# Cutting the last output block of a GeGLU kernel at 384 + 128 columns instead of 256 + 256

## Chip, cores, metric

One core of a Trainium2 chip. The metric is the device time of one execution in microseconds (us). A kernel is timed in rounds beside the kernel before on the same chip. A ratio is the mean time of one kernel's fast runs over the mean of the other's fast runs in the same rounds, so it is not quite the ratio of the medians that I quote; its 95% interval stands in brackets. Each run is marked fast or slow, by its time and the clock granted to TensorE.

## The reference

```python
# x: [32, 32, 1024]   w_gate, w_up: [1024, 3584]   w_down: [3584, 1024], bfloat16
def reference(x, w_gate, w_up, w_down):
    return (_gelu(x @ w_gate) * (x @ w_up)) @ w_down     # gelu in its tanh form
```

So there are 1024 tokens. A first product makes the gated hidden tensor `gT` (3584 x 1024, kept in SBUF). A second product multiplies it by `w_down`.

## The kernel before

The change touches the second product only. Each output block is 128 tokens by 512 columns. Its sum runs over 28 tiles of 128 rows: 28 pairs of a weight load (of a `gT` tile) and a matmul (which streams columns of `wd`). Then VectorE casts the block from PSUM to bfloat16, and SyncE (SP in the profile) issues a store. There are 8 x 2 blocks, and the very last one is already cut into two halves of 256 columns.

```python
    def mm2_block(tsl, dsl):
        out_ps = pspool.tile([P, dsl.stop - dsl.start], fp32, name="out_ps", tag="acc")
        for ft in range(FT):                                  # FT = 28
            nc.tensor.matmul(out_ps, lhsT=gT[:, ft, tsl], rhs=wd[:, ft, dsl],
                             start=(ft == 0), stop=(ft == FT - 1))
        o_sb = opool.tile([P, DB], bf16, name="o_sb", tag="o_sb")[:, : dsl.stop - dsl.start]
        nc.vector.tensor_copy(o_sb, out_ps)
        nc.sync.dma_start(out=of[tsl, dsl], in_=o_sb)

    for tt in range(NT):                                      # NT = 8, NDB = 2, DB = 512
        tsl = slice(tt * P, (tt + 1) * P)
        for db in range(NDB):
            if tt == NT - 1 and db == NDB - 1 and DB % 2 == 0:
                q = DB // 2
                for i in range(2):
                    mm2_block(tsl, slice(db * DB + i * q, db * DB + (i + 1) * q))
            else:
                mm2_block(tsl, slice(db * DB, (db + 1) * DB))
```

(Loads, warm-up matmuls and the first product with its elementwise work are cut; the change doesn't touch them.)

## Time and profile before

| | before |
|---|---|
| device time, median of the first 3 runs | 301.06 us (300.96 to 301.46) |
| span of the profiled execution | 298.9 us |
| first weight load of the second product | 198.24 us |
| first matmul of the last 512 columns to the last landing | 8.32 us |
| last landing to the end of the span | 1.42 us |

From the page of the kernel before, the span and the busy time of each engine:

```profile
span 298.9 us, 3462 instructions
...
PE 294.6 (99%) x1381; PEld 135.4 (45%) x1381; DVE 108.2 (36%) x241; ACT 97.6 (33%) x170; POOL 0.2 (0%) x4
...
PE 99%; DVE 0%; issue 0%
PE gate_ps L107 33%; PE out_ps L182 32%; PE up_ps L107 32%; PE warm_ps L73 1%; DVE o_sb L190 0%
```

PE is TensorE's matmuls and PEld its weight loads, which overlap them. The last two lines are the chain of work that ended last. It is TensorE nearly throughout. The Trainium skill warns ("Perfetto Trace Analysis", Identifying the Most-Contended Engine) that the busy share of matmuls is not a good measure of how close a kernel is to its limit, because matmuls are pipelined. This trace shows the pipelining: one matmul of 512 columns is recorded with 379 ns while the next starts 216 ns after it. (The section says that pipelined instructions look smaller in a trace; here the record is longer than the step.) I therefore work with start times.

The end of the kernel, grouped by shape (busy us, mean ns of one, then idle time before and who ended it), window 285 us to the end:

```profile
L182 PEld LDWEIGHTS <-gT 128*128 128x128 bf16 x74 | 7.2, 98 | 3.0
L182 PE MATMUL out_ps<-wd,gT 128*128 128x256 bf16 x56 | 6.3, 272 | 0.0
...
L190 DVE CAST o_sb<-out_ps 128x256 bf16<-128x256 f32 x2 | 0.8, 425 | 5.0 <-PE out_ps L182 5.0
L190 DVE CAST o_sb<-out_ps 128x512 bf16<-128x512 f32 x1 | 0.7, 693 | 5.4 <-PE out_ps L182 5.4
```

The cast waits for PE; no wait of PE for a cast is recorded. After the last matmul, the chain in order of time (start us, duration us), same kernel:

```profile
295.00 0.10 PEld L182 LDWEIGHTS <-gT 128*128 128x128 bf16 x1
295.42 0.42 DVE L190 CAST o_sb<-out_ps 128x256 bf16<-128x256 f32 x1 [2.63 <-PE out_ps L182]
295.87 0.33 SPq L191 DMA_DIRECT2D out_dram<-o_sb  x1
```

The last store of before, with its size and the time from issue to landing (the median that the view gives is of this one store):

```profile
out_dram<-o_sb SPq DMA_DIRECT2D x1, 64.0 KB, 1.6
```

Only what follows the last matmul is exposed: the cast, the issue of the store, its landing, and the closing work. This stretch is what the change is after.

### The profile page before, as it was taken

To read this page: it belongs to the slowest core of one execution; us is meant where nothing else is said; L and a number is where in the kernel's file an instruction comes from. 1 tells how busy PE (TensorE), PEld (TensorE's weight loads), DVE (VectorE), ACT (ScalarE), POOL (GpSimd) and SP (SyncE) were. 2 spreads that over 40 slices of the span, in tenths; PEclk is the share of its full clock that TensorE was granted. 3 is DMA by queue.
4 is the path that set the end of the run, shared out by engine and by line. 5 is a ranking of instruction groups with operands and counts; after the bars stand their busy time and mean duration, and the time that the engine had idled before them with its cause. 6 is when DMAs were issued, how large, how long until landed. Compare 5 with 4: busy or idle time off the path is not lost.

```text
span 298.9 us, 3462 instructions
## 1 busy us (share of the span) xinstructions
PE 294.6 (99%) x1381; PEld 135.4 (45%) x1381; DVE 108.2 (36%) x241; ACT 97.6 (33%) x170; POOL 0.2 (0%) x4
## 2 busy tenths in 40 slices
PE   8999999999999999999999999999999999999995
PEld 3444444444444444444444444444444444444454
DVE  0067654455554455554445554440010001000101
ACT  1086545544544544544544544530000000000000
POOL 0000000000000000000000000000000000000000
PEclk9999999999999999999999999999999999999999
DMA  7999996080026006200800000000001000100010
GB/s 175 265 305 378 377 365 246 1 279 3 0 83 197 2 0 190 91 2 1 277 5 2 0 0 2 0 0 18 20 18 35 18 20 18 35 20 18 18 35 21
DMA packets 29168, 26.44 MB, mean 88 GB/s; under 512 B 9056, under 2 KB 25568, under 8 KB 29152
## 3 DMA queue, kind: packets, MB, share of 16 engines
q1 hardware_dynamic: 28880, 25.96, 27.8%
q10 hardware_dynamic: 272, 0.26, 0.3%
q8 instruction: 11, 0.18, 0.2%
q14 instruction: 5, 0.04, 0.1%
HBM read 22.02 MB, written 2.10 MB: 81 GB/s over the span
## 4 chain that ended last, share of the span: by engine, by line
PE 99%; DVE 0%; issue 0%
PE gate_ps L107 33%; PE out_ps L182 32%; PE up_ps L107 32%; PE warm_ps L73 1%; DVE o_sb L190 0%
## 5 line engine op out<-in xcount | busy, mean ns | idle before, releaser
L107 PE MATMUL gate_ps<-xT,wg 128*128 128x512 bf16 x448 | 106.6, 380 | 0.0
L107 PE MATMUL up_ps<-xT,wu 128*128 128x512 bf16 x448 | 106.3, 379 | 0.0
L182 PE MATMUL out_ps<-wd,gT 128*128 128x512 bf16 (+1 forms) x476 | 96.9, 366 | 0.0
L182 PEld LDWEIGHTS <-gT 128*128 128x128 bf16 x476 | 46.6, 98 | 50.4
L107 PEld LDWEIGHTS <-wg 128*128 128x128 bf16 x448 | 43.9, 98 | 53.7 <-issue 1.1
L107 PEld LDWEIGHTS <-wu 128*128 128x128 bf16 x448 | 43.8, 98 | 52.9
L117 ACT ACTIVATE h<-gate_ps 128x512 bf16<-128x512 f32 x56 | 33.4, 597 | 54.9 <-PE gate_ps L107 54.8
L125 ACT ACTIVATE s<-z 128x512 bf16<-128x512 bf16 x56 | 35.3, 630 | 45.9 <-DVE z L123 45.9
L127 DVE TENSOR_TENSOR hu<-h,up_ps 128x512 bf16<-128x512 bf16 x56 | 38.2, 682 | 16.6 <-ACT h L117 16.6
L121 DVE TENSOR_SCALAR w<-sq 128x512 bf16<-128x512 bf16 x56 | 16.4, 294 | 74.3 <-ACT sq L119 74.3
L190 DVE CAST o_sb<-out_ps 128x512 bf16<-128x512 f32 (+1 forms) x17 | 11.2, 661 | 84.6 <-PE out_ps L182 84.6
L119 ACT ACTIVATE sq<-gate_ps 128x512 bf16<-128x512 f32 x56 | 33.1, 592 | 0.0
L128 DVE TENSOR_TENSOR gT<-hu,s 128x512 bf16<-128x512 bf16 x56 | 23.8, 426 | 10.5 <-ACT s L125 10.4
L123 DVE TENSOR_TENSOR z<-w,h 128x512 bf16<-128x512 bf16 x56 | 23.8, 425 | 1.8
L73 PE MATMUL warm_ps<-const-bfloat16-1.0 128*128 128x512 bf16 x9 | 4.0, 626 | 0.8 <-PEq L216 0.8
L73 PEld LDWEIGHTS <-const-bfloat16-1.0 128*128 128x128 bf16 x9 | 1.2, 137 | 2.7 <-issue 2.7
L117 ACT ACT_TABLE_LOAD x1 | 1.3, 1283 | 1.2 <-PEq L216 1.2
L125 ACT ACT_TABLE_LOAD x1 | 1.3, 1283 | 0.0
L216 POOL MEMSET const-bfloat16-1.0<- 128x1 bf16 x1 | 0.1, 102 | 0.0
L216 POOL MEMSET const-uint8-127<- 128x1 uint8 x1 | 0.1, 102 | 0.0
L216 POOL MEMSET const-float32-0.0<- 128x1 f32 x1 | 0.1, 99 | 0.2 <-issue 0.2
L216 POOL MEMSET const-float32-1.0<- 128x1 f32 x1 | 0.1, 99 | 0.0
## 6 DMA issues: line engine op xcount, KB each, us to landing
wd<-in_w_down_dram SPq DMA_DIRECT2D x7, 1024.0 KB, 12.6
wg<-in_w_gate_dram SPq DMA_DIRECT2D x6, 1024.0 KB, 5.2
wu<-in_w_up_dram SPq DMA_DIRECT2D x6, 1024.0 KB, 7.4
out_dram<-o_sb SPq DMA_DIRECT2D x15, 128.0 KB, 1.7
wu<-in_w_up_dram SPq DMA_DIRECT2D x4, 256.0 KB, 4.7
wg<-in_w_gate_dram SPq DMA_DIRECT2D x3, 256.0 KB, 4.7
wg<-in_w_gate_dram ACTq DMA_DIRECT2D x1, 256.0 KB, 2.9
out_dram<-o_sb SPq DMA_DIRECT2D x2, 64.0 KB, 2.0
```

The costliest lines, as they stand in the source:

```text
L73: nc.tensor.matmul(warm_ps, lhsT=ones_w, rhs=ones_m, start=True, stop=True)
L107: nc.tensor.matmul(ps, lhsT=wt[:, dt, :], rhs=xT[:, dt, t0 : t0 + tw], start=(dt == 0), stop=(dt == DT - 1),)
L117: nc.scalar.activation(h, gate_ps, ACT.Copy)
L119: nc.scalar.activation(sq, gate_ps, ACT.Square)
L121: nc.vector.tensor_scalar(w, sq, _C2A, _C2, ALU.mult, ALU.add)
L123: nc.vector.tensor_tensor(z, w, h, ALU.mult)
L125: nc.scalar.activation(s, z, ACT.Sigmoid)
L127: nc.vector.tensor_tensor(hu, h, up_ps, ALU.mult)
L128: nc.vector.tensor_tensor(gT[:, ft, t0 : t0 + tw], hu, s, ALU.mult)
L182: nc.tensor.matmul(out_ps, lhsT=gT[:, ft, tsl], rhs=wd[:, ft, dsl], start=(ft == 0), stop=(ft == FT - 1),)
L190: nc.vector.tensor_copy(o_sb, out_ps)
L216: nc = _bacc.Bacc("TRN2", target_bir_lowering=False, num_devices=1)
```

## The change

Its intent: make the last piece small, so that less cast and less store stand after the last matmul. The sum of columns is the same.

```diff
-            if tt == NT - 1 and db == NDB - 1 and DB % 2 == 0:
-                q = DB // 2
-                for i in range(2):
-                    mm2_block(tsl, slice(db * DB + i * q, db * DB + (i + 1) * q))
+            if tt == NT - 1 and db == NDB - 1 and DB > P:
+                cut = (db + 1) * DB - P
+                mm2_block(tsl, slice(db * DB, cut))
+                mm2_block(tsl, slice(cut, (db + 1) * DB))
```

The order of instructions on every engine stays; only shapes change: the widths of the last two runs of 28 matmuls, of their two casts and of their two stores.

## The prediction

> **What bounds the kernel now.** TensorE. The profile's engine table has PE busy 294.6 us of a 298.9 us span (99%), and the chain of waits is 99% PE, 32% of it the second product (out_ps). The granted clock is 1.0. Busy time overcounts overlapping matmuls, so I use starts: 512-column matmuls start every 216 ns and the 256-column ones of the last two blocks every 109.2 ns. That is N/2.4 + 2.5 ns, the warm spacing that the Trainium skill states ("TensorE: Matmul & The Clock Gate", Back-to-back issue gap); this trace agrees at both widths.
>
> The only exposed part is the tail. Instruction times before: last matmul starts at 295.112 us; the cast of 128x256 starts 0.31 us later and takes 0.425; the store is issued at 295.874, its first packet moves at 296.705, the last landing is at 297.431; closing work to 298.85.
>
> **What the change does.** Still 476 matmuls and loads, 17 casts and stores. The last block goes from 256+256 to 384+128 columns. Nothing before 289.1 us changes. No wait is added: the 384 block's cast and store issue finish before the last cast is due.
>
> Costs, as estimates from the measured spacing and durations:
> - Matmul stream: 28 x 162.5 + 27 x 55.8 ns to the last start against 55 x 109.2 ns: +0.05 us, provided that 128-column matmuls do stream at 55.8 ns.
> - End of the last matmul: 0.273 us falls to about 0.219: -0.05.
> - Last cast: 0.692 (512) and 0.425 (256) give 1.04 ns a column, so 0.29 for 128: -0.13.
> - Last store: 32 KB instead of 64 KB, 8 packets per DMA engine at about 17 ns instead of 27: -0.08 at best. Rows of 256 bytes fall under the 512-byte size that the skill names for full DMA rate ("DMA: Bandwidth & Descriptors", Specifications), so this may be lost.
>
> Sum: -0.2 us.
>
> **The risk: weight loads.** Each matmul needs its own weight load, whose record lasts 98 ns, longer than 55.8. If loads could not overlap each other, spacing would be about 100 ns and the last block 1.2 us longer: net +1.0 us. I think it is mostly latency: one warm load, after an idle PE near 18.9 us, is followed by its matmul 5 ns later and by the next load 15 ns later; at the start a cold load is followed by its matmul after 31 ns. So I give about 65-70% to spacing of 56 to 65 ns, the rest to 75 to 105 ns.
>
> **Prediction:** 300.9 us, range 300.4 to 301.9. Faster by over 2%: 0.5%; within 2%: 99%; slower by over 2%: 0.5%. The largest change I can argue for is 1 us, 0.4%.
>
> **What would show each step.** Right: 128-column matmuls start 55-65 ns apart; the last one starts near 295.2 us; the last cast is 0.29 us; last cast start minus last matmul start falls from 0.31 to about 0.26; the store from issue to last landing takes 1.5 us or less (1.56 before). Wrong: loads about 98 ns apart and the last matmul starting near 296.3 us; or a store clearly above 1.6 us; or a last cast not shorter.
>
> **What would make it wrong.** Loads that bound the last 28 matmuls; 256-byte rows landing slowly; an instruction fetch transfer (one of 16 KB stood at 293.1 us) falling in front of the last store; or run-to-run variation, as large as the effect (301.0 to 301.5 in the three runs).

## The result, and the profile after

First timing: after 300.88 us median (300.75 to 301.17, 6 runs), before 301.29 us (300.96 to 301.88, 6 runs), ratio 0.9986 [0.9973, 0.9999]. Within 2%, and within the predicted range.

From the page of the kernel after:

```profile
span 298.9 us, 3436 instructions
...
PE 293.4 (98%) x1355; PEld 134.3 (45%) x1381; DVE 108.1 (36%) x241; ACT 97.6 (33%) x170; POOL 0.2 (0%) x4
...
PE 97%; DMA 1%; issue 1%; DVE 0%
```

26 matmul records are missing (1355 of 1381), while all 1381 weight loads are there. The profile loses such records now and then; the lower PE share is no finding. I count with weight loads where it matters.

The end of the kernel after, grouped by shape, 285 us to the end:

```profile
L182 PEld LDWEIGHTS <-gT 128*128 128x128 bf16 x75 | 6.2, 98 | 4.3
...
L182 PE MATMUL out_ps<-wd,gT 128*128 128x384 bf16 x28 | 4.7, 326 | 0.0
L182 PE MATMUL out_ps<-wd,gT 128*128 128x128 bf16 x28 | 1.7, 219 | 0.0
...
L190 DVE CAST o_sb<-out_ps 128x384 bf16<-128x384 f32 x1 | 0.6, 558 | 3.9 <-PE out_ps L182 3.9
L190 DVE CAST o_sb<-out_ps 128x128 bf16<-128x128 f32 x1 | 0.3, 291 | 1.0 <-PE out_ps L182 1.0
```

And in order of time:

```profile
294.74 1.63 SPq L191 DMA_DIRECT2D out_dram<-o_sb  x2
294.79 0.89 PE L182 MATMUL out_ps<-wd,gT 128*128 128x128 bf16 x13
294.96 0.54 PEld L182 LDWEIGHTS <-gT 128*128 128x128 bf16 x9
295.72 0.29 DVE L190 CAST o_sb<-out_ps 128x128 bf16<-128x128 f32 x1 [1.01 <-PE out_ps L182]
```

The SPq line covers both store issues, the last one from 296.03 us. That last store:

```profile
out_dram<-o_sb SPq DMA_DIRECT2D x1, 32.0 KB, 1.4
```

Thirteen matmuls of 128 columns take 0.89 us, of which the last one's own duration is 0.22: the twelve steps between them are 56 ns each. The weight loads are recorded with 98 ns and start 56 ns apart, so they overlap one another.

Notice that both spans read 298.9 us, though the time fell. The lines of the second product's weight loads (count, duration ns min/median/max, first and last start in us), before:

```profile
L182 PEld LDWEIGHTS <-gT x476: 97/98/98, 198.2 to 295.0; 128*128 128x128 bf16 x159
```

and after:

```profile
L182 PEld LDWEIGHTS <-gT x476: 97/98/98, 198.5 to 295.4; 128*128 128x128 bf16 x159
```

In the profiled execution of after the second product began 0.29 us later, before any changed instruction. What the change did is therefore read from the tail, the stretch from the first matmul of the last 512 columns on. These are instruction times of the traces, in us:

| piece of the tail | before | after | difference | predicted |
|---|---|---|---|---|
| first to last matmul start | 6.004 | 6.058 | +0.054 | +0.05 |
| last matmul start to cast start | 0.310 | 0.257 | -0.053 | -0.05 |
| last cast | 0.425 | 0.291 | -0.134 | -0.13 |
| cast end to store issue | 0.027 | 0.027 | 0 | 0 |
| store issue to last landing | 1.557 | 1.440 | -0.117 | -0.08 at best |
| tail | 8.32 | 8.07 | -0.25 | -0.2 |
| closing work, last landing to end of span | 1.42 | 1.42 | 0 | 0 |

In the 14 traces the second product begins between 197.95 and 198.88 us, whatever the kernel; the standard deviation is 0.29 us. That is the size of the effect, so one timing cannot settle it. A better figure is the time from the first weight load of the second product to the end of the span, which leaves the head (everything before the second product) out. I call it the second part below. It is 100.61 us before and 100.35 us after. Of before there is this one trace; of after there are three, with second parts within 0.02 us of each other though two of them are from different chips.

### The profile page after: what moved, and what is told of

It reads as the page before. It is cut to its first block, busy times and chain, and to the rows that moved or that the text cites. A ratio compares the mean times of both kernels' runs of the same rounds, so it can differ in the third digit from the quotient of the medians.

```text
span 298.9 us, 3436 instructions
## 1 busy us (share of the span) xinstructions
PE 293.4 (98%) x1355; PEld 134.3 (45%) x1381; DVE 108.1 (36%) x241; ACT 97.6 (33%) x170; POOL 0.2 (0%) x4
## 4 chain that ended last, share of the span: by engine, by line
PE 97%; DMA 1%; issue 1%; DVE 0%
PE gate_ps L107 32%; PE out_ps L182 32%; PE up_ps L107 32%; DMA xT<-in_x_dram 1%; DVE o_sb L190 0%
## 5 line engine op out<-in xcount | busy, mean ns | idle before, releaser
L182 PE MATMUL out_ps<-wd,gT 128*128 128x512 bf16 (+2 forms) x468 | 96.5, 366 | 0.4
L182 PEld LDWEIGHTS <-gT 128*128 128x128 bf16 x476 | 45.5, 98 | 51.6
L190 DVE CAST o_sb<-out_ps 128x512 bf16<-128x512 f32 (+2 forms) x17 | 11.2, 660 | 84.4 <-PE out_ps L182 79.1
```

## The experiments

Theory A: the time falls because a shorter last piece shortens only what stands exposed after the last matmul. Rival B: the 0.4 us of the first timing is how the heads happened to run. Rival C: the matmul stream decides, and splits only cost. A further rival, on the risk that the prediction named: the 28 short matmuls streamed well only because they were few.

A summary first. "Second part" is as defined above. The device time exceeds the recorded span by about 2 us (time that the trace doesn't show). Every timed run lists its span, so this excess can be had for all runs of a kernel: it averages 1.98 us for before (1.81 to 2.10 over its runs) and differs a little from kernel to kernel. The ratio that the traces give is 1 + (difference of the second part + difference of the mean excess) / 301.

| kernel | tail us | closing us | second part, against before, us | mean excess us | ratio that these give | ratio measured |
|---|---|---|---|---|---|---|
| after (first) | 8.07 | 1.42 | -0.26 | 1.97 | 0.9991 | 0.9986 [0.9973, 0.9999] |
| after_again | 8.08 | 1.42 | -0.24 | 2.02 | 0.9993 | 0.9997 [0.9985, 1.001] |
| after_third | 8.08 | 1.42 | -0.24 | 1.97 | 0.9992 | 0.9987 [0.9976, 0.9999] |
| e1_whole, 512 | 8.66 | 1.13 | +0.04 | 1.86 | 0.9997 | 0.9999 [0.9985, 1.0013] |
| e6_whole_padded, 512 | 8.66 | 1.03 | -0.06 | 1.84 | 0.9993 | 0.9998 [0.9985, 1.0012] |
| e2_reversed, 128 + 384 | 8.51 | 1.42 | +0.18 | 1.98 | 1.0006 | 1.0004 [0.9991, 1.0016] |
| e3_448_64 | 8.50 | 1.42 | +0.18 | 1.94 | 1.0004 | 1.0 [0.9988, 1.0013] |
| e4_store_256 | 8.19 | 1.42 | -0.14 | 2.02 | 0.9997 | 0.9994 [0.998, 1.0008] |
| e7_448_64_act | 8.10 | 1.19 | -0.45 | 2.02 | 0.9986 | 0.9988 [0.9974, 1.0002] |
| e8_448_64_early | 8.05 | 1.43 | -0.19 | 2.17 | 1.0000 | 1.001 [0.9998, 1.0023] |
| e5_all_128 | - | 0.83 | +2.52 | 1.82 | 1.0078 | 1.0077 [1.006, 1.0094] |
| e9_after_merged | 8.08 | 1.12 | -0.55 | 1.89 | 0.9979 | 0.9975 [0.9959, 0.9991] |
| e10_after_merged2 | 8.09 | 0.90 | -0.76 | 2.19 | 0.9982 | 0.9976 [0.9963, 0.9989] |

The ratio that the traces give lies inside the measured interval for every kernel. That is a weak test, since an interval is about as wide as 0.7 to 1 us and so wider than most of the effects; the traces carry the argument. The outputs are right.

### after_again and after_third: the change repeated

No edit.

> The changed kernel once more, so that every later run has it beside it. 'Tail' below is the time from the first matmul of the last 512 output columns to the last landing of the last store: 8.32 us in the profile of before, 8.07 us in the first profile of after. Theory A (a shorter last piece shortens only what is exposed after the last matmul): tail 8.07 us again, within 0.05; time 0.25 us under before. Theory B (the 0.4 us of the first timing is how the head of the kernel happened to run, and the tail adds nothing that is seen): time equal to before within 0.1 us, although the tail is shorter in the profile.

> The changed kernel a third time, for the size of its gain and beside the two merged ones. Theory A: from the first matmul of the second product to the end of the span 0.25 us less than before, as in its other two profiles; time 0.25 us (ratio 0.9992) under before, within noise of about 0.3 us that comes from the head.

Measured: tails of 8.08 and 8.08 us, second part 0.24 us shorter than before both times. Times 301.10 us (before 301.05) and 300.92 us (before 301.18); ratios as in the table. Theory A holds in the traces three times out of three. The timings alone are weaker: the middle one contains "no difference", and all three contain the 0.9991 to 0.9993 that the traces give. The three ratios average 0.9990. Rival B is right only about the size of the first timing: of its 0.4 us, 0.25 is the change by the traces, and the rest I put down to the runs.

### e1_whole: no split

```diff
-                for i in range(2): mm2_block(... 256 columns ...)
+                mm2_block(... 512 columns ...)
```

> The last block in one piece of 512 columns, no split. Theory A: stream to the last start 27 x 216 ns = 5.83 us (0.17 us less than before), then 0.42 us to the cast, cast 0.69, store 1.70 us from issue to landing: tail 8.67 us, so 0.35 us slower than before and 0.60 us slower than after. Theory B: equal to before. A theory C, that the matmul stream decides: 0.17 us faster than before.

Measured: the tail came out as theory A had it, 8.66 us (5.83 to the last start, 0.42, cast 0.69, store 1.70). The end of it, by shape:

```profile
L190 DVE CAST o_sb<-out_ps 128x512 bf16<-128x512 f32 x2 | 1.4, 692 | 10.7 <-PE out_ps L182 10.7
```

But the time was equal to before: 300.95 against 301.05 us, ratio 0.9999. As a forecast of the time this was a miss. The trace shows where most of the 0.34 us came back: the closing work after the last landing took 1.13 us instead of 1.42. The mean excess was 0.12 us smaller too. Theory C falls with the same tail: the stream was 0.18 us shorter than in before, as C had it, and what stood after it grew by 0.52. So the closing work is not a constant, and something other than the tail had changed with the split. That led to e6, and later to e9 and e10.

### e2_reversed: the same pieces, long one last

```diff
-                mm2_block(384 columns); mm2_block(128 columns)
+                mm2_block(128 columns); mm2_block(384 columns)
```

> The same two pieces in reverse order, 128 and then 384: the same matmuls, casts and stores as after, only the last piece is the long one. Theory A: tail 5.95 + 0.36 + 0.56 + 0.03 + about 1.63 = 8.53 us, 0.46 us slower than after and 0.2 us slower than before. A rival, that the gain comes from the kinds of pieces (fewer ns per matmul, cheaper forms) and not from which is last: equal to after.

Measured: tail 8.51 us, against 8.53 expected. The casts of its last three blocks (512, 128 and 384 columns) are

```profile
L190 DVE CAST o_sb<-out_ps x3: 293/558/691, 289.3 to 295.4; 128x512 bf16<-128x512 f32 x1, 128x128 bf16<-128x128 f32 x1, 128x384 bf16<-128x384 f32 x1
```

and the last of them is the one of 384 columns. The second part is 0.44 us longer than in after, with the same set of instructions and the same closing work of 1.42 us. So it is the place of the short piece that counts, not its kind. The time, 301.09 us and ratio 1.0004, lies on the expected side but inside the noise.

### e3_448_64: the cut moved further

```diff
-                384 + 128
+                448 + 64
```

> The cut moved further: 448 and then 64 columns. If weight loads still don't bind at 64 columns: matmuls 29 ns apart, tail 6.09 + 0.23 + 0.23 + 0.03 + about 1.40 = 7.97 us, 0.1 us faster than after. If a weight load needs more than 29 ns of its own (40 ns, say), the last block is 0.3 us longer and the tail about 8.26 us, 0.2 us slower than after. In either case the 448-column piece's cast and store issue end close to when the last piece wants them, so a short wait of the last cast or of the last store issue may show.

Measured: tail 8.50 us, later than either forecast. The two questions came apart. Weight loads still don't bind. These are the groups by shape, from 294.7 to 296 us:

```profile
L182 PE MATMUL out_ps<-wd,gT 128*128 128x64 bf16 x28 | 1.0, 193 | 0.0
L182 PEld LDWEIGHTS <-gT 128*128 128x128 bf16 x28 | 1.0, 98 | 0.2
```

28 loads and 28 matmuls within 1.0 us; in the instruction times they start 29 ns apart, as forecast. The loss is in the store. In order of time:

```profile
295.03 0.62 DVE L190 CAST o_sb<-out_ps 128x448 bf16<-128x448 f32 x1 [4.61 <-PE out_ps L182]
295.69 1.27 SPq L191 DMA_DIRECT2D out_dram<-o_sb  x2
295.85 0.22 DVE L190 CAST o_sb<-out_ps 128x64 bf16<-128x64 f32 x1 [0.19 <-PE out_ps L182]
```

The two issues together occupy SP's queue for 1.27 us: the first took 0.33, the second, 0.42 us after it, 0.85. A 16 KB instruction fetch, one packet, ran from 295.33 to 296.57 us, and the packets of the 448-column store began at 296.52. Its slowest packet took 211 ns, where the same store's slowest in e8 took 49. The last packet ended 0.73 us after the first began, against 0.45 to 0.46 us in e7 and e8. Two explanations were left: the two issues are too close on one queue (Q), or the fetch holds up the stores (F). (That these fetches are PE's I infer from their spacing: about 27.6 us in before, where a load and a matmul start every 216 ns, and 7.15 us in e5_all_128 below, where they start every 55.9 ns. That is about 256 PE instructions a fetch in both.)

### e7_448_64_act and e8_448_64_early: which of the two

```diff
# e7_448_64_act: e3's cut, and the last store from ACT's queue
-        nc.sync.dma_start(out=of[tsl, dsl], in_=o_sb)
+        eng = nc.scalar if tsl.stop == N and dsl.stop == D else nc.sync
+        eng.dma_start(out=of[tsl, dsl], in_=o_sb)
# e8_448_64_early: e3's cut, SP's queue; the first block of the second product in two PSUM halves,
# one store: 56 more PE instructions, so that the fetch comes earlier
```

> 448 and 64 columns, the last store issued from ACT's queue instead of SP's. In e3_448_64 matmuls did run 29 ns apart, but the issue of the last store, 0.42 us after the one before it, took 0.85 us instead of 0.33. Theory Q (two issues close together on one queue): the issue takes about 0.33 to 0.42 us here and the tail is 7.98 us. Theory F (the 16 KB instruction fetch of 1.24 us, which stood there at that time, holds up the store): the issue or the landing is again about 0.5 us late, tail about 8.5 us.

> 448 and 64 columns on SP's queue as in e3_448_64, but the first output block of the second product is also computed in two halves of 256 columns (one store): 56 more instructions on PE, 0.07 us more of matmul stream, so that the last instruction fetch comes earlier than in e3_448_64, by about 28 matmul pairs. Theory F: the fetch is over before the last store, its issue takes 0.33 us, tail 7.98 us. Theory Q: the issue takes 0.85 us again, tail 8.49 us.

Measured in e8_448_64_early: the fetch ran from 289.63 to 290.51 us, long before the end; the issues are again 0.42 us apart on the same queue, and the second took 0.38 us.

```profile
295.09 0.81 SPq L191 DMA_DIRECT2D out_dram<-o_sb  x2
295.26 0.23 DVE L190 CAST o_sb<-out_ps 128x64 bf16<-128x64 f32 x1 [0.19 <-PE out_ps L182]
```

So close issues alone cost 0.05 us, and the 0.5 us needed the fetch: F, in this trace. But a late fetch alone is not enough either. In after_again, after_third and e9_after_merged a fetch overlapped the packets of the 384-column store (slowest 222, 222 and 204 ns), which landed 2.03 to 2.33 us after its issue; yet the last store, issued 1.30 us after that one, landed within 1.44 to 1.45 us of its own issue, as in after. The 0.5 us of e3_448_64 came from the late fetch and the close second issue together. In e7_448_64_act the issue took 0.36 us and the tail was 8.10 us, but there the fetch (294.91 to 295.85 us) had ended before the packets began at 296.13, so that run doesn't separate the two. Whether the late fetch would also hold up a store on another queue stays open.

The trace of before supports F with no edit at all: its store of 292.82 us overlapped a fetch (293.12 to 293.99), its slowest packet took 186 ns, and it landed 2.35 us after issue, where the last store of the same size took 1.56. That landing was not exposed.

Both expected a tail of 7.98 us and got 8.05 and 8.10: the last store's packets began 0.88 to 0.89 us after its issue instead of 0.83, just when those of the 448-column store had ended (11 and 32 ns later). It seems that at 64 columns the last store runs into the one before it (the timing fits, no run tests it), and the 0.1 us that the shorter piece should have brought over after shrank to at most 0.03. The time of e8 was 301.23 us (ratio 1.001), slower than its trace suggests: its excess over the span was 2.13 to 2.22 us in all six runs, 0.19 us above that of before. Why this kernel loses time outside the recorded span I don't know.

### e4_store_256: the store's share alone

```diff
 # matmuls and casts of 384 and 128 columns as in after, into one output tile
-                stores of 384 and 128 columns
+                stores of 256 and 256 columns
```

> Matmuls and casts of after (384 and 128), but the stores cut at 256: the last store carries 64 KB in rows of 512 bytes, as in before. It measures the store's share alone: last store 1.56 us from issue to landing instead of 1.44, the rest of the tail as in after, tail 8.19 us. If short rows cost something at landing, the 1.44 us would be matched or beaten here.

Measured: last store 1.557 us from issue to landing, tail 8.19 us, both as expected. Its two stores:

```profile
out_dram<-o_sb SPq DMA_DIRECT2D x2, 64.0 KB, 1.6
```

The two halves of the gain are thus told apart: 0.117 us of the 0.25 is the smaller store, the rest is the cast (0.134), with the matmul terms cancelling (+0.054 and -0.053). Rows of 256 bytes cost nothing at landing: their packets take 18 ns, those of 512 bytes 27, of 1024 bytes 47.

### e5_all_128: the weight loads, 64 times over

```diff
-                mm2_block(tsl, slice(db * DB, (db + 1) * DB))
+                for c in range(db * DB, (db + 1) * DB, P):
+                    mm2_block(tsl, slice(c, c + P))
```

> Every block of the second product in pieces of 128 columns (64 casts and stores of 32 KB instead of 17): the load question of the prediction, 64 times over. If a weight load streams at 56 ns for good (A): 1792 matmuls x 55.85 ns = 100.1 us instead of 96.9, time 3.2 us over before (ratio 1.011), less the shorter tail. If the 28 matmuls of after ran at 56 ns only because PE's queue held them ready (rival): spacing falls to 80 or 98 ns after the first block, and the time rises by 46 to 79 us.

Measured: 303.58 against 301.18 us, ratio 1.0077 [1.006, 1.0094]. The loads of the second product:

```profile
L182 PEld LDWEIGHTS <-gT x1792: 97/98/98, 198.3 to 298.4; 128*128 128x128 bf16 x200
```

1792 loads in 100.16 us are 55.9 ns each, to the end. The rival is out: the short stream holds without the help of a filled queue. The stream grew by 3.40 us (from 96.76), as forecast within 0.2; the stretch after the last load shrank by 0.88 us, of which 0.59 is closing work, which I had not foreseen.

### e6_whole_padded: what goes with the closing work

```diff
 # e1_whole, and the store of the block before the last issued in two halves of 256 columns
```

> One piece of 512 columns again, with one store of the block before it issued in two halves, so that SP issues 17 stores as in before. In e1_whole the tail was 0.34 us longer than in before (as theory A had it) but the closing work after the last landing took 1.13 us instead of 1.42, and the time was equal. If the closing work goes with the number of instructions on SP (theory S): tail 8.66 us as in e1_whole, closing work 1.42 us, time 0.3 us over before, about 301.4. If it went with the missing split itself: closing 1.13 us and time equal to before.

Measured: tail 8.66 us as in e1_whole, closing work 1.03 us, time 300.92 against 301.04 us (ratio 0.9998). Theory S as I had written it fell, for the closing work did not go back to 1.42. But the padding had not done what I meant. The extra store waits for one semaphore, not two, so SP has 82 traced instructions instead of 83. By that count the traces line up. In before, after, e2, e3, e4 and e8 there are 83 instructions of SP, and in each SP stops between two of its closing instructions. In e1 and e7 there are 81, and the stop stands two closing instructions later. From instruction times (us, SP only; "drain" and "wait" are the trace's DRAIN and EVENT_SEMAPHORE):

```
before (83)              e1_whole (81)            e10 below (79)
297.601  drain           297.917  drain           297.312  drain
298.068  drain  <- stop  297.977  drain           297.381  drain
298.329  wait            298.130  wait            297.534  wait
298.421  drain           298.608  drain  <- stop  297.625  drain
298.790  wait            298.884  wait            298.001  wait
```

The usual step from the first to the second is 0.06 us; here it is 0.47. In e1 the stop falls where SP would wait for other engines in part anyway, which hides some of it.

### e9_after_merged and e10_after_merged2: the closing work moved on purpose

```diff
 # e9: the stores of the first two blocks of the second product merged into one of 256 KB
 # e10: the first four blocks' stores merged in pairs
+            if tt == 0:                    # e10: tt < 2
+                ... both casts into o_big[128, 1024] ...
+                nc.sync.dma_start(out=of[tsl, :], in_=o_big)
```

> after, with the stores of the first two output blocks of the second product merged into one of 256 KB: 16 stores instead of 17, and the same PE instructions as after. Over the runs so far the closing work after the last landing was 1.42 us where the trace has 83 instructions of SP, 1.03 us with 82 and 1.13 to 1.19 us with 81, because one gap of about 0.4 us stands at a fixed place of SP's instruction stream. By that (theory S, mended): 81 instructions here, closing 1.13 us, tail 8.07 us as in after, time 0.3 us under after. If the closing had gone with PE's instructions or with the split: 1.42 us.

> after, with the first four output blocks' stores merged in pairs: 15 stores, 79 instructions of SP. By theory S the gap of SP falls behind the last instruction of the span: closing work at most 1.0 us, tail 8.07 us, so 0.4 us under after and 0.65 us under before, time about 300.4 us. If S is wrong: closing 1.42 us and time equal to after.

Measured: the tails stayed at 8.08 and 8.09 us, the closing work fell to 1.12 us (81 instructions) and 0.90 us (79), as the mended theory had it. PE's instructions and the split are those of after, so neither is what moves the stop. Times: 300.55 us, ratio 0.9975 [0.9959, 0.9991], and 300.54 us, 0.9976 [0.9963, 0.9989], beside before at 301.18. These two have the lowest ratios, and both are below before clear of noise. Against after in the same rounds (300.92 us) they are 0.4 us faster by the medians, but the intervals overlap.

e10 was forecast below e9 and was not: its closing work is 0.22 us shorter, but its excess over the span is 2.11 to 2.28 us in its six runs, on average 0.30 us above that of e9. So of the 0.52 us that e10's closing work lost against after, about 0.2 came back behind the last recorded instruction. The stop pushed out of the span is the obvious suspect, but nothing in the trace shows that time, and e8_448_64_early has as large an excess (2.17 us) with its stop inside the span.

That a stop stands at a fixed place of SP's instruction stream is shown by five counts. With 81, 82 and 83 instructions it stands before the 80th traced instruction of SP, in all 12 such traces; with 79 there is no 80th, and the closing work has no stop. The fifth count is the strongest: e5_all_128 has 177 and no stop in its closing work (0.83 us). There the step from the 79th to the 80th falls in the middle of the second product, at 230.28 us, and takes 0.77 us, where the same step takes 0.38 in the next blocks. That it is a fetch of instructions is only a guess: an 8 KB fetch is recorded near that instruction in each of these traces, but it starts after the stop has ended (298.70 us in before, against 298.07 for the 80th instruction; 231.10 us in e5_all_128, against 231.05).

## Why the prediction was right

- **Bound by TensorE, with only the tail exposed.** Right. e2_reversed keeps every instruction and moves only the order of the two pieces, and the second part grows by 0.44 us.
- **Matmul stream +0.05 us, end of the last matmul -0.05.** Right: +0.054 and -0.053.
- **Last cast -0.13.** Right: -0.134, from 425 to 291 ns.
- **Last store "-0.08 at best".** The direction was right and the term too small: -0.117, shown alone by e4_store_256. The packets gave -0.09 (from the first packet to the end of the last 0.354 us before, 0.262 after); the rest came between the last packet and the last landing. The caution about rows of 256 bytes was needless.
- **The risk: weight loads.** The argument from two records, that 98 ns is mostly latency, was right. Loads 56 ns apart over 1792 pairs (e5_all_128) and 29 ns apart over 28 (e3_448_64) show it. The prediction took its spacing from a formula that the page itself gives for isolated matmuls (first point of the last section) and did not mention the larger figure that the page gives for pairs at 128 columns; the measurement sided with the formula.
- **Sum -0.2 us, 300.9 us.** The tail fell by 0.25 us; 300.88 us was measured. That the medians agree so closely is luck: in its two later timings the same kernel had 301.10 and 300.92 us, beside before at 301.05 and 301.18. The range of 300.4 to 301.9 would have held "no change" as well, so it is the steps, not the time, that bear the prediction out.
- **Fetch "falling in front of the last store".** It did not happen in after, whose fetch ended at 295.48 us, 1.4 us before the first packet of the last store. In e3_448_64 a fetch ran into the last two stores, and the tail was about 0.5 us longer than forecast.

What the prediction did not consider is that the closing work can change when the number of SP's instructions does. It kept the number at 83, so nothing came of it here. In e1_whole the same omission spoiled a forecast.

## What to carry to other kernels

When one engine is busy throughout, as here, look at what stands after its last instruction: make the last piece small, but not so small that its store comes close behind the one before it (here 128 columns gained 0.25 us over 256; 64 gained at most 0.03 more, and with a late fetch lost 0.42 against 128). Short matmuls with a new weight load each cost little: 128 columns in 55.9 ns, against 54 for a quarter of a 512-column one. For effects below the run-to-run noise compare stretches of the trace that start behind the noise, and check that the end of the program, after the last landing, and the time outside the span are the same in both kernels.

## What the Trainium skill lacked or had wrong

- "TensorE: Matmul & The Clock Gate", Back-to-back issue gap: it gives, for streams of weight load and matmul pairs, about 81 ns a matmul at 128 columns and 131 at 512, and calls N/2.4 + 2.5 the gap of an isolated matmul. In these runs pairs follow N/2.4 + 2.5 at every width: 29 ns at 64 columns, 55.9 at 128 (1792 in a row), 109.2 at 256, 162.5 at 384, 216 at 512.
- The same page, LDWEIGHTS: it gives the time of a load as P/1.2, which makes an estimate of 107 ns for 128 columns. Neither that section nor the one on weight-path modes after it gives the spacing of bf16 loads that follow one another. The trace records 98 ns, and loads start as little as 29 ns apart.
- "DMA: Bandwidth & Descriptors", Specifications: it asks for at least 512 bytes and speaks of read-modify-write below. For stores of 128 rows to HBM no step shows there: packets of 128, 256, 512, 768 and 1024 bytes take 13, 18, 27, 36 and 47 ns.
- I found no page that says that fetches of PE's instructions (16 KB each, about every 27.6 us at 512 columns, 0.9 to 1.8 us long in these traces) delay stores that they meet: landing 2.35 us instead of 1.56 in before, and a store issue of 0.85 us instead of 0.33 in e3_448_64.
- I found no page that mentions the stop of about 0.4 us in SP's closing instructions, before the 80th of SP's traced instructions: 1.42, 1.03, 1.12 to 1.19 and 0.90 us of closing work with 83, 82, 81 and 79; with 79, the device time exceeds the span by 2.19 us on average instead of 1.98.
